# Local and global attention with a routed expert layer on one core: the split weights as sixteen tiles, expert 1's loads in quarters, and two changes in the attention's order

## The chip, the cores and the metric

The kernel is one program on one core of a Trainium2 chip. The metric is the device time of one execution in microseconds, taken as the median of several runs. A profile of one execution was taken besides; its times are counted from the first instruction of the span.

## The reference, cut to what matters

Attention of 8 batches and 8 heads with 512 local and 32 global rows per head gives x, 4352 rows of 512. Each row of x goes to one of 8 experts, chosen by the largest logit against `expert_emb`:

```python
out_g = np.matmul(sm(s_g), v_all)                 # globals look at all keys
a_l = sm(np.concatenate([s_lg, s_ll], axis=-1))   # locals: the globals and a window of 32 either side
x = attn_out.transpose(0, 2, 1, 3).reshape(B * S, H * D)
...
expert_idx = np.argmax(logits, axis=1)
for e in range(E):
    mask = expert_idx == e
    h = np.maximum(x[mask] @ w1[e], 0.0)
    out[mask] = gate_w[mask, None] * (h @ w2[e])
```

`w1[e]` is 512x1024 and `w2[e]` is 1024x512, all in float32.

## The kernel before, in words

**Attention and routing.** 32 steps, four for each batch. Every step has a slot in a plan (`at(g, phase, ...)`, L886 to L968): in slot g the phases are carried out in the order of the numbers at L890, apart from a few that `slot` (L999) puts elsewhere. TensorE computes scores, transposes and values; VectorE the row maxima (`maxima`, L525) and the normalisation of a step's values into x (`normed`, L589 to L597: three instructions on the PSUM tile `po`); ScalarE the exponentials and the copies. The globals' part of a batch is `g_scores`, `g_exps`, `g_turned`, `g_take` and `g_values` (L600 to L682); `g_values` ends in three VectorE instructions (L672 to L675) that wait for TensorE. GpSimd scatters the finished rows of x into the DRAM table `xs`, ordered by expert, and the last rows of each expert's part are filled up by `fill_rest` (L1121): expert 0's from SyncE's queue (SP), the seven others from GpSimd's. Two blocks of 128 rows of expert 0 are computed early with plain float32 matmuls (`early_block`, L200).

**The expert stage.** The remaining rows are worked in items of 128 rows of one expert (`item`, L1276); 36 of them ran in the profiled execution. Float32 products are made from two parts: a rounded part H and the rest L, of the weights (`WH`, `WL`) and of the activations (`xH`/`xL`, `hH`/`hL`), and three matmuls for each (HH, HL, LH). `WH` and `WL` were one tile each, [128, 4, 4096]: two experts by two halves (w1, w2). ScalarE casts `stg` into `WH` and VectorE subtracts it to get `WL`, in pieces of 512 columns (`w_parts`, L1293); one half, 8 pieces, for each item, for the expert that comes next. `first_parts` (L1206) does the same for expert 0 in pieces of 1024 columns. Where a piece's place is known only at run time, its address comes from a register (`ds(ra, 1)`), and the framework that sets the semaphores then orders it by tiles.

An item w is, in TensorE's order: `up(0)` and `up(1)`, 12 matmuls of 128x128x512 each (x times w1, two halves of h), then the two `down`, 12 matmuls each, of the item before it. h needs a transpose through DRAM: ScalarE makes relu (`relu`, L1252) and puts it to `hd` with a DMA of its own queue (`put_h`, L1259), SP loads it back as `hq` (`get_h`, L1263), VectorE turns it in 32x32 blocks into `hk` (L167), and ScalarE and VectorE split it into `hH` and `hL`. An expert's weights come into two stages, `stg0` for w1 and `stg1` for w2, by `load_w` (L1226) with two DMAs of 1 MB on SP's queue, some of which are skipped by a condition. SP's queue is in the order of the program: what waits at its head holds up all behind it. Items 0, 1 and 2 and the rest have orders written out by hand (L1341 to L1391). At the end `declare_no_dep` takes out the orders between the two slots that the framework can't see.

Of the kernel before, what the change touches and what calls it, by code (L numbers as in the profile page):

```python
# [107 lines left out]
def tile_kernel(ctx: ExitStack, tc: tile.TileContext, qk, va, emb, tau, wraw, cst, out):  # L108
# [29 lines left out]
    xT1 = const.tile([P, DM], F32, name="xT1")  # L138
    sums = [const.tile([P, 4 + NE], F32, name=f"ce{i}") for i in range(4)]
# [60 lines left out]
    def early_block(x, h, hT, ob, acc, acc2):  # L200


        def turn(src):
            o = acc()
            for c in range(4):
                transpose(o[:, c * P : (c + 1) * P], src[:, c * P : (c + 1) * P], ident)
            return o

        st = {}

        def begin(xT):
            st["xT"] = xT
            turn_blocks(xT[:, :DM], x[:, :DM])

        def up(nh, ks):
            if ks[0] == 0:
                st["g", nh] = acc()
                if nh == 0:
                    st["h"], st["hT"] = h(), hT()
            for k in ks:  # L220
                c = k * 1024 + nh * 512
                matmul(
                    st["g", nh], st["xT"][:, k * P : (k + 1) * P], cols(st0[0], c, c + 512), start=(k == 0), stop=(k == 3)
                )
            if ks[-1] == 3:
                nc.scalar.activation(st["h"][:, nh * 512 : (nh + 1) * 512], st["g", nh], AF.Relu)

        def half(nh):
            nc.scalar.copy(st["hT"][:, nh * 512 : (nh + 1) * 512], turn(st["h"][:, nh * 512 : (nh + 1) * 512]))

        def down(ks):
            if ks[0] == 0:
                st["g2"] = acc2()
            for k in ks:
                matmul(
                    st["g2"],
                    st["hT"][:, k * P : (k + 1) * P],
                    cols(st0[1], k * 512, (k + 1) * 512),
                    start=(k == 0),
                    stop=(k == 7),  # L240
                )
# [21 lines left out]
        lambda: hq,  # L263
# [5 lines left out]
    with ExitStack() as actx:  # L269
# [634 lines left out]
        for b in range(NB):  # L904
# [116 lines left out]
        def fetch_early():  # L1021
# [5 lines left out]
            for i, x in enumerate((eb[0], xn1)):  # L1027
# [5 lines left out]
                    lambda: eb[3],  # L1033
# [68 lines left out]
    wp.tile([P, 104], F32, name="gap_wp")  # L1102
    WH = wp.tile([P, 4, 4096], F32R, name="WH")
    WL = wp.tile([P, 4, 4096], F32R, name="WL")
    WH2 = WH.rearrange("p (s h) n -> p s (h n)", s=2)
    WL2 = WL.rearrange("p (s h) n -> p s (h n)", s=2)

# [3 lines left out]
    hq = hp.tile([P, DF], F32, name="hq")  # L1111
    hqs = [hq[:, :DM], hq[:, DM:]]
# [6 lines left out]
    firsts = []  # L1119

    def fill_rest(e):  # L1121

        eng = nc.gpsimd if e else nc.sync
        r = eng.value_load(runi[:1, e : e + 1], min_val=e * CAP, max_val=e * CAP + NT)
        ins = eng.dma_start(xs[ds(r, P), :], fill)
        for f in fills + scat + early + (firsts if e else []):
# [79 lines left out]
    def first_parts(hf, c):  # L1206

        cs = slice(c * 1024, (c + 1) * 1024)
        src = cols(st0[hf], cs.start, cs.stop)
        nc.scalar.copy(WH[:, hf, cs], src)  # L1210
        nc.vector.tensor_tensor(WL[:, hf, cs], src, WH[:, hf, cs], ALU.subtract)

# [13 lines left out]
    def load_w(w):  # L1226
        r = entry(nc.sync, 1, w, 2 * NE - 1)
        src = wraw[ds(r, 1), :, :].rearrange("a p (c n) -> p (a c) n", n=WRUN)
        for n in range(2):
            cs = slice(2 * n, 2 * n + 2)  # L1230
            new = {} if w < 2 else {"cond": entry(nc.sync, 4 + n, w, 1)}
            nc.sync.dma_start(st0[w % 2][:, cs, :WRUN], src[:, cs, :], **new)

# [42 lines left out]
    def item(w, pend):  # L1276
# [9 lines left out]
        if w == 0:  # L1286
            todo = []
        elif w == 1:
            todo = [(*held[0], c) for c in range(8)] + [(*held[1], c) for c in range(3)]
        elif w == 2:  # L1290
            todo = [(*held[1], c) for c in range(3, 8)] + todo

        def w_parts(n):  # L1293
            for _ in range(min(n, len(todo))):
# [7 lines left out]
        def product(o, a, W, col, start=False, stop=False):  # L1302
            return nc.tensor.matmul(o.unsqueeze(1), a, W[:, ds(rp, 1), col : col + 512], start=start, stop=stop)  # L1303

        def up(nh):
            g = ps_1.tile([P, 512], F32, name="g1")
            for k in range(4):
                col = k * 1024 + nh * 512
                reads.append(product(g, xH[:, k, :], WH2, col, start=k == 0))
                reads.append(product(g, xH[:, k, :], WL2, col))  # L1310
                reads.append(product(g, xL[:, k, :], WH2, col, stop=k == 3))
# [4 lines left out]
        def down(nh):  # L1316
# [3 lines left out]
            for k in ks:  # L1320
                made.append(product(g, hH[:, k, :], WH2, 4096 + k * 512, start=k == 0))
                made.append(product(g, hH[:, k, :], WL2, 4096 + k * 512))
            for k in ks:
                made.append(product(g, hL[:, k, :], WH2, 4096 + k * 512, stop=k == 7))
# [16 lines left out]
        if w == 0:  # L1341
            load_w(1)
            send_h(0, ga)
            send_h(1, up(1))
            get_h(w, 0)
            get_h(w, 1)
        elif w == 1:
            w_parts(2)
            send_h(0, ga)
            w_parts(1)  # L1350
# [4 lines left out]
            w_parts(1)  # L1355
            send_h(1, gb)
            get_h(w, 0)
            turn_h(1)
# [3 lines left out]
            w_parts(4)  # L1362
            load_w(w + 1)
            w_parts(3)
            get_h(w, 1)
            reads.extend(pend["down"](1))
        else:
# [15 lines left out]
            if w == 2:  # L1383
                w_parts(2)
                load_w(w + 1)
# [10 lines left out]
        for i, (v, c, m) in enumerate(made):  # L1396
            for u, d, o in last_made + made[:i]:
                if o.ins.engine != m.ins.engine and ((v - u) % 2 or (v == u and c != d)):
                    tc.declare_no_dep(m.ins, o.ins, reason="another half or other columns")
# [17 lines left out]
    with tc.manual_schedule():  # L1417
        nc.vector.tensor_copy(runi, run[:1])
        fill_rest(0)
        for w in range(2):  # L1420
            firsts.extend(load_x(w))
        for e in range(1, NE):
            fill_rest(e)
        tab["tab"], nitem = table()
        parts = [(hf, c) for hf in range(2) for c in range(4)]
        for i, f in enumerate(block):
            if i:
                f()
            for _ in range((2, 0, 1, 0, 1, 1, 0, 2, 0, 0, 0)[i]):
                first_parts(*parts.pop(0))  # L1430
            if i == 8:
                load_w(0)
                turn_x(0)
                split_x(0)
                first_parts(*parts.pop(0))
                turn_x(1)
                split_x(1)
        pend = {}
# [96 lines left out]
```

## Time and profile before

| | us |
|---|---|
| median of 3 runs | 712.75 |
| the runs | 713.24, 708.89, 712.75 |
| the profiled execution | 715.34 |
| its span, first to last instruction | 713.7 |
| TensorE busy | 648.0 (91%) |
| VectorE busy | 541.4 (76%) |
| ScalarE busy | 471.3 (66%) |

The profiled execution took 715.34 us, of which 1.6 lie outside its span. Its stages, by the first matmul of each: attention to about 237 us, the routing's end and the early blocks to 273, items 0 to 3 to 327, items from the fifth on to 685, and the last item with its output to the end. Busy TensorE doesn't mean TensorE at its peak: matmuls overlap, and what counts is the distance from one start to the next. In the timeline's rows a bracket holds the idle time ahead of the row and what ended it; "ACTq" and "SPq" are DMA issues; the chain of waits goes back from the last instruction and gives, in order of time, what each step waited for.

### The profile page before, as it was taken

How to read it: one execution, taken by the hardware profiler on the slowest of the kernel's cores; microseconds unless marked ns; L12 is line 12 of the kernel's file. 1: busy time of each engine (PE TensorE's matmuls, PEld its weight loads, DVE VectorE, ACT ScalarE, POOL GpSimd, SP SyncE). 2: the span in 40 equal slices, each digit the busy share in tenths (PEclk: the TensorE clock that was granted, in tenths of full speed). 3: DMA queues.
4: the chain of work that ended last, by engine and by line, in shares of the span. 5: the costliest groups of instructions: out<-in, count | busy, mean ns of one | idle time of the engine just before them, and what ended most of it. 6: DMA issues, size and time to landing. Idle time of an engine off the chain costs nothing.

```text
span 713.7 us, 23574 instructions
## 1 busy us (share of the span) xinstructions
PE 648.0 (91%) x7423; PEld 497.4 (70%) x7425; DVE 541.4 (76%) x1716; ACT 471.3 (66%) x954; POOL 96.6 (14%) x179
## 2 busy tenths in 40 slices
PE   8789879878887899779999999999999999998994
PEld 4567667656676546657777787777878787776783
DVE  2758779789777684778888888787888878867882
ACT  4676767758667244667777776777777776766771
POOL 2011122122212350000100101010110101010101
PEclk9899999999999899889999999999999999999998
DMA  8898899879899259765545577678777787764451
GB/s 258 308 255 257 260 286 275 259 238 297 274 278 290 78 191 313 213 216 167 159 135 144 137 256 202 197 232 255 239 214 208 229 259 220 228 191 128 136 150 40
DMA packets 125148, 154.71 MB, mean 217 GB/s; under 512 B 15881, under 2 KB 81545, under 8 KB 125016
## 3 DMA queue, kind: packets, MB, share of 16 engines
q1 hardware_dynamic: 80680, 114.48, 54.3%
q10 hardware_dynamic: 38016, 18.88, 9.0%
q0 software_dynamic: 6320, 19.71, 7.5%
q8 instruction: 69, 1.13, 0.6%
q14 instruction: 63, 0.52, 0.2%
HBM read 161.36 MB, written 40.94 MB: 283 GB/s over the span
## 4 chain that ended last, share of the span: by engine, by line
PE 37%; DVE 19%; DMA 14%; ACT 12%; issue 11%; ACTq 3%; SPq 2%; DVEq 1%; POOL 0%; another core or an unknown queue 0%; POOLq 0%
DVE WL L1299 14%; PE g L1303 10%; PE pt L198 8%; PE po L195 7%; ACT WH L1298 6%; DMA hd<-h 6%; PE pt L195 6%; PE s_ps L195 5%; ACT h L1253 4%; DMA hq<-hd 3%; DMA raw<-in_qk_dram 3%; ACTq L1261 3%; DMA stg<-in_wraw_dram 1%; DVE hk L167 1%; SPq L1220 1%
## 5 line engine op out<-in xcount | busy, mean ns | idle before, releaser
L1299 DVE TENSOR_TENSOR WL<-stg,WH 128x512 f32 (+1 forms) x288 | 197.8, 689 | 65.0 <-ACT WH L1298 50.2
L1298 ACT CAST WH<-stg 128x512 f32 (+1 forms) x288 | 177.6, 620 | 41.9 <-ACT h L1253 35.2
L1303 PE MATMUL g<-WL,xH 128*128 (+1 forms) x288 | 117.8, 409 | 8.7 <-DVE WL L1299 6.7
L1303 PE MATMUL g<-WH,hH 128*128 (+1 forms) x288 | 114.3, 397 | 10.0 <-ACT hH L1235 10.0
L1303 PE MATMUL g<-WH,xH 128*128 (+1 forms) x288 | 114.3, 397 | 4.4 <-ACT WH L1298 4.3
L1303 PE MATMUL g<-WH,xL 128*128 (+1 forms) x288 | 114.0, 396 | 0.0
L1303 PE MATMUL g<-WL,hH 128*128 (+1 forms) x288 | 114.0, 396 | 0.0
L175 POOL DMA_INDIRECT out_dram<-ob x37 | 36.0, 974 | 407.6 <-DVE xk L167 354.7
L552 ACT ACTIVATE pb<-pb,nm 128x128 f32<-128x128 f32 x256 | 80.1, 395 | 11.0 <-DVE nm L535 11.0
L1303 PE MATMUL g<-WH,hL 128*128 (+1 forms) x288 | 78.1, 393 | 0.0
L1303 PEld LDWEIGHTS g<-WL,xH 128*128 128x128 f32 x288 | 55.1, 191 | 32.7 <-DVE WL L1299 22.0
L1303 PEld LDWEIGHTS g<-WH,hH 128*128 128x128 f32 x288 | 55.2, 192 | 22.8 <-ACT hH L1235 6.5
L1303 PEld LDWEIGHTS g<-WH,xH 128*128 128x128 f32 x288 | 55.0, 191 | 18.9 <-ACT WH L1298 6.2
L1303 PEld LDWEIGHTS g<-WL,hH 128*128 128x128 f32 x288 | 55.2, 192 | 11.5
L1303 PEld LDWEIGHTS g<-WH,hL 128*128 128x128 f32 x288 | 55.0, 191 | 11.7
L1303 PEld LDWEIGHTS g<-WH,xL 128*128 128x128 f32 x288 | 55.3, 192 | 10.9 <-DVE xL L1236 0.4
L195 PE MATMUL s_ps<-raw 64*32 64x128 f32 (+1 forms) x1792 | 49.6, 287 | 12.5 <-issue 7.9
L167 DVE STREAM_TRANSPOSE hk<-hq 128x512 f32<-128x512 f32 x72 | 50.3, 698 | 12.7 <-DMA hq<-hd 8.9
L195 PE MATMUL po<-vt,pT 128*32 128x65 f32 x2048 | 46.1, 231 | 11.0 <-issue 9.7
L1235 ACT CAST hH<-hk 128x512 fp32r<-128x512 f32 x72 | 44.5, 618 | 14.9 <-DVE hk L167 14.6
L564 ACT COPY pT<-pt 128x512 f32<-128x512 f32 x64 | 34.4, 588 | 28.2 <-PE pt L198 28.0
L1253 ACT ACTIVATE h<-g 128x512 f32<-128x512 f32 x72 | 43.0, 597 | 14.7 <-PE g L1303 12.9
(200 smaller groups left out, 879.3 us busy)
## 6 DMA issues: line engine op xcount, KB each, us to landing
stg<-in_wraw_dram SPq DMA_DIRECT2D x74, 1024.0 KB
vt<-in_va_dram SPq DMA_DIRECT2D x96, 260.0 KB
hd<-h ACTq DMA_DIRECT2D x72, 256.0 KB
hq<-hd SPq DMA_DIRECT2D x72, 256.0 KB
raw<-in_qk_dram SPq DMA_DIRECT2D x56, 304.0 KB
xr<-xs SPq DMA_DIRECT2D x152, 64.0 KB
vt<-in_va_dram SPq DMA_DIRECT2D x32, 130.0 KB
stg<-in_wraw_dram SPq DMA_DIRECT2D x16, 256.0 KB
```

Of the source, the lines that this page charges most:

```text
L167: nc.vector.transpose(xT.rearrange("p (k t n) -> p t k n", k=4, t=4), x.rearrange("p (t k n) -> p t k n", t=4, k=4))
L175: nc.gpsimd.indirect_dma_start(out=out[:, :], out_offset=bass.IndirectOffsetOnAxis(ap=ob[:, DM : DM + 1].bitcast(U32), axis=0), in_=ob[:, ...
L195: return counted(nc.tensor.matmul(out, lhsT, rhs, start=start, stop=stop), 4 if lhsT.dtype == F32 else 2)
L198: return counted(nc.tensor.transpose(out, in_, eye), 2)
L552: nc.scalar.activation(pb[:, cs], pb[:, cs], AF.Exp, bias=nm[:, n : n + 1], scale=-1.0)
L564: nc.scalar.copy(pT, state["tp", g, grp])
L1235: nc.scalar.copy(tH, x)
L1253: nc.scalar.activation(hs[nh].rearrange("p (g k n) -> p k g n", g=4, k=4), g.rearrange("p (k g n) -> p k g n", k=4, g=4), AF.Relu,)
L1261: nc.scalar.dma_start(hd, hs[nh].rearrange("p (g n) -> p g n", g=4))
L1298: a = nc.scalar.copy(WH[:, ds(ra, 1), cs], s3)
L1299: b = nc.vector.tensor_tensor(WL[:, ds(rv, 1), cs], s3, WH[:, ds(rv, 1), cs], ALU.subtract)
L1303: return nc.tensor.matmul(o.unsqueeze(1), a, W[:, ds(rp, 1), col : col + 512], start=start, stop=stop)
```

## The change

`WH` and `WL` become eight tiles each of [128, 4, 512], one per 512 columns (columns of w1 for k = 0..3 and the two halves of h, so that tile c = 2k + nh holds what `up(nh)` reads for k, and `down` reads tile k of w2). `first_parts` goes by 512 columns, tiles 0, 2, 4, 6 first. The declarations at the item's end are cut accordingly. `hq` becomes two tiles. Expert 1's weights come in quarters of 512 KB (`first_w`), the first set ahead of item 0 and the second around item 0's loads of h; item 0 casts four pieces, item 1 eight (eleven before), item 2 twelve (thirteen before); in items 1 and 2 `load_w` stands between the two loads of h. All eight fills stand on SP ahead of the first loads of x. `normed` moves into the phase of `g_values`, ahead of it, and the last copy of the last batch's globals into the phase before. Two spare columns are set anew so that the tiles begin where they did.

```diff
-            at(g + 2, NORM, normed, g)
+            at(g + 2, GVAL, normed, g)
...
-                at(g, LATE, g_take, b, part)
+                at(g, BACK if b == NB - 1 and part == 2 else LATE, g_take, b, part)
...
-    WH = wp.tile([P, 4, 4096], F32R, name="WH")
-    WL = wp.tile([P, 4, 4096], F32R, name="WL")
+    WH = [wp.tile([P, 4, 512], F32R, name=f"WH{c}") for c in range(8)]
+    WL = [wp.tile([P, 4, 512], F32R, name=f"WL{c}") for c in range(8)]
...
-    hq = hp.tile([P, DF], F32, name="hq")
-    hqs = [hq[:, :DM], hq[:, DM:]]
+    hqs = [hp.tile([P, DM], F32, name=f"hq{nh}") for nh in range(2)]
...
-        eng = nc.gpsimd if e else nc.sync
-        r = eng.value_load(runi[:1, e : e + 1], min_val=e * CAP, max_val=e * CAP + NT)
-        ins = eng.dma_start(xs[ds(r, P), :], fill)
+        r = nc.sync.value_load(runi[:1, e : e + 1], min_val=e * CAP, max_val=e * CAP + NT)
+        ins = nc.sync.dma_start(xs[ds(r, P), :], fill)
...
+    def first_w(w, lo, hi):
+        src = wraw[2 + w].rearrange("p (c n) -> p c n", n=WRUN)
+        for n in range(lo, hi):
+            nc.sync.dma_start(st0[w][:, n, :WRUN], src[:, n, :])
...
-                a = nc.scalar.copy(WH[:, ds(ra, 1), cs], s3)
-                b = nc.vector.tensor_tensor(WL[:, ds(rv, 1), cs], s3, WH[:, ds(rv, 1), cs], ALU.subtract)
+                a = nc.scalar.copy(WH[c][:, ds(ra, 1)], s3)
+                b = nc.vector.tensor_tensor(WL[c][:, ds(rv, 1)], s3, WH[c][:, ds(rv, 1)], ALU.subtract)
...
         if w == 0:
-            load_w(1)
             send_h(0, ga)
+            w_parts(2)
             send_h(1, up(1))
             get_h(w, 0)
+            first_w(1, 0, 1)
             get_h(w, 1)
+            first_w(1, 1, 4)
+            w_parts(2)
         elif w == 1:
             w_parts(2)
             send_h(0, ga)
-            w_parts(1)
+            w_parts(2)
             turn_h(0)
             split_h(0)
             gb = up(1)
             reads.extend(pend["down"](0))
-            w_parts(1)
             send_h(1, gb)
             get_h(w, 0)
+            load_w(w + 1)
             turn_h(1)
             split_h(1)
             turn_x(w + 1)
             split_x(w + 1)
             w_parts(4)
-            load_w(w + 1)
-            w_parts(3)
             get_h(w, 1)
...
-        fill_rest(0)
-        for w in range(2):
-            firsts.extend(load_x(w))
-        for e in range(1, NE):
+        for e in range(NE):
             fill_rest(e)
+        load_x(0)
+        load_x(1)
...
             if i == 8:
-                load_w(0)
+                first_w(0, 0, 4)
```

On SP, in items 0 and 1 (`hd_58`, `hd_59` are the halves of item 0's h, `stg_90` is w2's stage before, `hq` what VectorE turns), before:

```order
L158 DMA gt_5757<-xs 128x1x2
L1232 DMA stg_90<-in_wraw_dram 128x2x1024 x2
L1264 DMA hq<-hd_58 128x512
L1264 DMA hq<-hd_59 128x512
L1220 TENSOR_LOAD tab
```

and now (w2's stage is `stg_91`, in four pieces):

```order
L159 DMA gt_5772<-xs 128x1x2
L1265 DMA hq_5776<-hd_58 128x512
L1233 DMA stg_91<-in_wraw_dram 128x1024
L1265 DMA hq_5777<-hd_59 128x512
L1233 DMA stg_91<-in_wraw_dram 128x1024 x3
L1216 TENSOR_LOAD tab
```

Both loads of h have moved ahead of all but a quarter of w2's load.

On TensorE, at the start of a later item's `up(0)`, with the semaphores that each row waits for (another engine's name: that engine has got so far), before:

```order
L1303 MATMUL g1_6675<-WH_5751,xH1_5766 128x512 [waits PE_49,Activation_49]
...
L1303 MATMUL g1_6675<-WL_5752,xH1_5766 128x512 [waits DVE_49]
...
L1303 MATMUL g1_6675<-WH_5751,xL1_5768 128x512
...
L1303 MATMUL g1_6675<-WH_5751,xH1_5766 128x512
...
L1303 MATMUL g1_6675<-WL_5752,xH1_5766 128x512
```

and now:

```order
L1305 MATMUL g1_6711<-WH0_5752,xH1_5782 128x512 [waits PE_49]
...
L1305 MATMUL g1_6711<-WL0_5760,xH1_5782 128x512
...
L1305 MATMUL g1_6711<-WH2_5754,xH1_5782 128x512 [waits Activation_49]
...
L1305 MATMUL g1_6711<-WL2_5762,xH1_5782 128x512 [waits DVE_49]
...
L1305 MATMUL g1_6711<-WH4_5756,xH1_5782 128x512 [waits Activation_49]
```

One wait each for ScalarE and VectorE at the item's first two matmuls has become pairs of waits at tiles 2, 4 and 6, and another pair at tile 7 in `up(1)`. (VectorE's own row for a piece of `WL` waited for VectorE and ScalarE, with two register instructions ahead; now it waits for ScalarE alone, with one.)

On VectorE, in an attention slot with `g_values` (`rs`, `xt` are `normed`'s, `rg`, `on` those of `g_values`), before:

```order
L672 TENSOR_SCALAR rg<-pt 128x1
L673 RECIPROCAL rg<-rg 128x1
L675 TENSOR_SCALAR on<-pt,rg 128x64
L594 TENSOR_SCALAR rs<-po 128x8
L595 RECIPROCAL rs<-rs 128x8
L597 TENSOR_TENSOR xt_163<-po,rs 128x4x4x32
```

and now:

```order
L595 TENSOR_SCALAR rs<-po 128x8
L596 RECIPROCAL rs<-rs 128x8
L598 TENSOR_TENSOR xt_164<-po,rs 128x4x4x32
L673 TENSOR_SCALAR rg<-pt 128x1
L674 RECIPROCAL rg<-rg 128x1
L676 TENSOR_SCALAR on<-pt,rg 128x64
```

The normalisation has moved ahead of the three instructions that wait for the globals' matmuls.

## Rows read from the trace of the kernel before

**Rows 1.** Stretches: us, busy time (instructions) by engine, PEclk, DMA share, GB/s.
```profile
236.60:273.00 36.40, 36.24 (x192) 18.29 (x192) 28.14 (x118) 15.55 (x25) 14.52 (x19) 0.94 0.49 152
273.00:326.90 53.90, 44.74 (x168) 35.33 (x169) 35.63 (x57) 31.45 (x54) 2.99 (x3) 0.87 0.74 236
326.90:685.50 358.60, 349.22 (x1490) 277.92 (x1489) 292.19 (x466) 256.06 (x434) 30.12 (x31) 1.00 0.66 197
```

**Rows 2.** Chain of waits within one item: start us, us, what.
```profile
361.84 2.80 PE g L1303 x11
...
369.22 0.70 DVE WL L1299
...
373.15 0.50 PE g L1303
```

**Rows 3.** Timeline of TensorE, items 0 to 4.
```profile
272.97 0.50 PE L1303 MATMUL g<-WH,xH 128*128 128x512 f32 x1
...
289.65 0.79 PE L1303 MATMUL g<-WH,hH 128*128 128x512 f32 x1 [5.23 <-ACT hH L1235]
...
297.94 0.39 PE L1303 MATMUL g<-WH,xH 128*128 x1
...
303.38 0.39 PE L1303 MATMUL g<-WH,hH 128*128 128x512 f32 x1
...
311.53 0.50 PE L1303 MATMUL g<-WH,xH 128*128 x1 [2.55 <-ACT WH L1298]
313.42 0.79 PE L1303 MATMUL g<-WL,xH 128*128 x1 [1.39 <-DVE WL L1299]
...
326.94 0.39 PE L1303 MATMUL g<-WH,xH 128*128 x1
```

**Rows 4.** Timeline of VectorE: seven pieces at fixed places, five at places from a register.
```profile
294.84 4.30 DVE L1299 TENSOR_TENSOR WL<-stg,WH 128x512 fp32r<-128x512 f32 x7
...
369.22 3.88 DVE L1299 TENSOR_TENSOR WL<-stg,WH 128x512 f32 x5 [0.81 <-ACT WH L1298]
```

**Rows 5.** Timeline of ScalarE in the item of rows 2.
```profile
364.67 0.60 ACT L1253 ACTIVATE h<-g 128x512 f32<-128x512 f32 x1 [0.27 <-PE g L1303]
...
368.57 3.23 ACT L1298 CAST WH<-stg 128x512 f32 x5 [0.54 <-ACT h L1253]
```

**Rows 6.** Chain of waits, whole span: start us, us, what.
```profile
277.50 6.88 DMA hd<-h
...
327.39 2.80 PE g L1303 x11
...
444.79 7.21 DMA hd<-h
452.06 2.33 DMA hq<-hd
...
464.25 5.50 DMA stg<-in_wraw_dram
470.90 2.80 DMA hd<-h
...
685.98 2.79 PE g L1303 x11
```

**Rows 7.** Timeline of SP's queue around items 0 and 1.
```profile
254.25 0.39 SPq L1125 DMA_DIRECT2D xs<-fill  x1
263.54 2.17 SPq L156 DMA_DIRECT2D xr<-xs  x4
...
276.25 4.64 SPq L1232 DMA_DIRECT2D stg<-in_wraw_dram  x2
284.44 3.48 SPq L1264 DMA_DIRECT2D hq<-hd  x2
```

**Rows 8.** Waits, whole span: who, for whom, us in total, times, longest us.
```profile
DVE rg L672 <- PE pt L195: 16.9, 12, 2.7
...
PE pt L198 <- DVE lg L748: 3.1, 1, 3.1
```

More of the change, by code (lines that the diff above doesn't have):

```diff
@@ L138, in tile_kernel @@
     xT1 = const.tile([P, DM], F32, name="xT1")
+    const.tile([P, 8], F32, name="gap_c")
     sums = [const.tile([P, 4 + NE], F32, name=f"ce{i}") for i in range(4)]
@@ L228, in half @@
         def half(nh):
-            nc.scalar.copy(st["hT"][:, nh * 512 : (nh + 1) * 512], turn(st["h"][:, nh * 512 : (nh + 1) * 512]))
+            nc.scalar.copy(st["hT"][nh], turn(st["h"][:, nh * 512 : (nh + 1) * 512]))
         def down(ks):
@@ L1118, in tile_kernel @@
     fills = []
[L1119 removed]
     def fill_rest(e):
[L1123 to L1126 removed]
+        r = nc.sync.value_load(runi[:1, e : e + 1], min_val=e * CAP, max_val=e * CAP + NT)
+        ins = nc.sync.dma_start(xs[ds(r, P), :], fill)
+        for f in fills + scat + early:
             tc.declare_no_dep(ins.ins, f.ins, reason="disjoint rows")
@@ L1206, in first_parts @@
     def first_parts(hf, c):
[L1208 to L1211, printed above, removed]
+        src = cols(st0[hf], c * 512, (c + 1) * 512)
+        nc.scalar.copy(WH[c][:, hf], src)
+        nc.vector.tensor_tensor(WL[c][:, hf], src, WH[c][:, hf], ALU.subtract)
     last_made = []
@@ L1286, in item @@
         if w == 0:
-            todo = []
+            todo = todo[:4]
         elif w == 1:
-            todo = [(*held[0], c) for c in range(8)] + [(*held[1], c) for c in range(3)]
+            todo = [(*held[0], c) for c in range(4, 8)] + [(*held[1], c) for c in range(4)]
         elif w == 2:
-            todo = [(*held[1], c) for c in range(3, 8)] + todo
+            todo = [(*held[1], c) for c in range(4, 8)] + todo
         def w_parts(n):
@@ L1307, in up @@
             for k in range(4):
[L1308 to L1311, printed above, removed]
+                c = 2 * k + nh
+                reads.append(product(g, xH[:, k, :], WH2[c], 0, start=k == 0))
+                reads.append(product(g, xH[:, k, :], WL2[c], 0))
+                reads.append(product(g, xL[:, k, :], WH2[c], 0, stop=k == 3))
             return g
@@ L1362, in item @@
             w_parts(4)
+            get_h(w, 1)
+            reads.extend(pend["down"](1))
+        elif w == 2:
+            turn_x(w + 1)
+            turn_h(0)
+            split_x(w + 1)
+            split_h(0)
+            turn_h(1)
+            send_h(0, ga)
+            w_parts(2)
+            split_h(1)
+            gb = up(1)
+            reads.extend(pend["down"](0))
+            send_h(1, gb)
+            w_parts(2)
+            get_h(w, 0)
             load_w(w + 1)
-            w_parts(3)
+            w_parts(8)
             get_h(w, 1)
@@ L1397, in item @@
             for u, d, o in last_made + made[:i]:
-                if o.ins.engine != m.ins.engine and ((v - u) % 2 or (v == u and c != d)):
-                    tc.declare_no_dep(m.ins, o.ins, reason="another half or other columns")
+                if c == d and (v - u) % 2:
+                    tc.declare_no_dep(m.ins, o.ins, reason="another half")
         last_made[:] = made
@@ L1418, in tile_kernel, with slices @@
         nc.vector.tensor_copy(runi, run[:1])
-        fill_rest(0)
-        for w in range(2):
-            firsts.extend(load_x(w))
-        for e in range(1, NE):
+        for e in range(NE):
             fill_rest(e)
+        load_x(0)
+        load_x(1)
         tab["tab"], nitem = table()
-        parts = [(hf, c) for hf in range(2) for c in range(4)]
+        parts = [(0, c) for c in (0, 2, 4, 6, 1, 3, 5, 7)] + [(1, c) for c in range(8)]
+        def slices(n):
+            for _ in range(n):
+                first_parts(*parts.pop(0))
         for i, f in enumerate(block):
@@ L1428, in tile_kernel @@
                 f()
-            for _ in range((2, 0, 1, 0, 1, 1, 0, 2, 0, 0, 0)[i]):
-                first_parts(*parts.pop(0))
+            slices((4, 0, 2, 0, 2, 2, 0, 0, 0, 0, 0)[i])
             if i == 8:
-                load_w(0)
+                first_w(0, 0, 4)
                 turn_x(0)
                 split_x(0)
-                first_parts(*parts.pop(0))
+                slices(2)
                 turn_x(1)
                 split_x(1)
+                slices(4)
         pend = {}
```

26 lines of the change are left out of this document (12 added, 14 removed).

## The prediction

> **What bounds the kernel now.** I read the table of stretches first [rows 1]: from 326.9 to the end of the items TensorE is busy in 349.22 of 358.6 us at a full granted clock. That looks like a bound, but busy time counts stalled matmuls too, so I looked at distances from start to start. Where nothing holds it, TensorE does 24 matmuls in 303.38 − 297.94 = 5.44 us [rows 3], 0.227 each; an item has 48, so it could take 10.88. The 31 items between the starts at 327.39 and 685.98 [rows 6] took 358.6/31 = 11.57 each, and the undisturbed one of [rows 2], from 361.84 to 373.15, took 11.31. So TensorE loses 0.69 per item, 21.3 us in all, and the stage's limit is something else.
>
> The chain inside one item [rows 2] says what: `up(0)`, then the casts, then the last piece of `WL` at the end of the run that starts at 369.22, and only behind it the next item's first matmul, at 373.15. In [rows 4] that run of five ends at 373.10, 0.05 before. Since `WL` is one tile, the next `up(0)` waits for the eighth piece though it reads the first. ScalarE's relu at 364.67 waited in turn for TensorE [rows 5]. This is a ring: `up(0)` → relu → `WH` → `WL` → `up(0)`.
>
> Two smaller losses lie ahead of it. From 273 to 326.9 the granted clock is 0.87, a mean over its two levels (1.2 and 2.4 GHz) [rows 1], and TensorE stands 5.23 us until h's first part comes [rows 3]; seven half items of 5.44 (38.1) take 54.0. In the attention VectorE waits 16.9 us in 12 places for the globals' matmuls, while TensorE's wait for VectorE at the routing is 3.1 once [rows 8].
>
> **The change part by part.** The profiled execution took 715.34, of which 713.7 are span; the median is 712.75. I make the sum against 715.34 and take 2.6 off.
>
> *Sixteen tiles, steady items.* `up(0)` reads tiles 0, 2, 4 and 6, three matmuls (0.68) each. The seven pieces of [rows 4] start (4.30 − 0.69)/6 = 0.60 apart; call the end of piece 7 T. Piece 6 is ready at T − 0.6 and wanted 2.04 behind the item's start, piece 4 at T − 1.8 and wanted at 1.36, piece 2 at T − 3.0 and wanted at 0.68. The item may start at the latest of T − 2.64, T − 3.16 and T − 3.68: 2.6 us sooner than now, and only 0.4 are needed to close the gap to 10.88. The ring through ScalarE, with its idle 0.27 gone, is 11.31 − 0.27 = 11.04 if nothing else changes. `WL` also loses its wait for VectorE itself and one register instruction. At register places the pieces now start (3.88 − 0.69)/4 = 0.80 apart, at fixed places 0.60; ScalarE's `WH` (3.23 − 0.62)/4 = 0.65. With 0.60 to 0.65 four steps give back 0.6 to 0.8, and the ring is 10.2 to 10.4, under TensorE's 10.88.
>
> The rows show that pieces without a wait on their own engine start 0.60 apart though each lasts 0.69, so the wait and the registers are the 0.20 [rows 4]. Against that stands the Trainium skill, VectorE: DVE Perf Modes, section "The DRAIN you can't avoid": the next operation can't issue until the pipe is empty, and a semaphore behind each operation "costs nothing extra". By it the step would stay 0.80 and the ring 11.04, which would take 31 × 0.16 = 5 us off the gain; the trace disagrees, with 0.60.
>
> What remains above 10.88 is h's trip through DRAM. When no weights are loading, `hd` takes 2.80; when they are, 7.21, with `hq` 2.33 behind [rows 6]. With relu, turn and split at 0.6 to 0.7 each that is an estimated 11.7, some 0.8 more than an item has. If this strikes once for each of the six later experts it is 5 us, 0.16 an item. So 11.04 per item and 31 × 0.53 = 16.5 us gained. Bounds: 21.3 if TensorE never waits, 12 if the slow items keep the 0.26 that they have above 11.31 now (31 × (11.57 − 11.18), with a little for restarts).
>
> *Items 0 to 3.* Now 2 MB stand on SP before h's loads: `stg` issued at 276.25, `hq` only at 284.44 [rows 7], and the first `hd` takes 6.88 [rows 6]. Then both loads of h go ahead of most of w2. With 2.80 and 2.33 for 6.88 and 3.48, h is there 5.2 sooner, which would end all of the 5.23 idle; as w1's quarters are still in flight I leave 1.3, a gain of 3.9. Without that stop the clock shouldn't fall: the stretch from 289.65 to 297.94 [rows 3] becomes 5.44 for 8.29, gain 2.85. Item 1's second half took 311.53 − 303.38 = 8.15, 2.55 of it waiting for `WH`; by tiles it would be 5.44, gain 2.7. From 311.53 to 326.94 are 15.4 us for 10.88, gain 4.5. Together 14. The casts are no fewer (32 pieces before item 3), so I take 12; the lower bound is 4, the idle time alone. The fifth item would start near 315 instead of 326.94.
>
> *Quarters.* Four DMAs of 512 KB for two of 1 MB. The nearest row is one 1 MB piece, 5.50 [rows 6]; four quarters that ran one behind another at that would be 22 us and late (rival B); overlapping like the pair at 276.25 [rows 7] they cost SP two more issues, hidden, as SP only waits then. I take nothing; worst 8 us. By the Trainium skill, DMA: Bandwidth & Descriptors, section "Measured (HBM→SBUF, 128 partitions, SWDGE, issued from GpSimd)", DMAs should be batched to 1 MiB or more; no row here has a 512 KB weight load, and my sum does not lean on the rule.
>
> *The fills on SP.* Seven more, each one issue (0.39 [rows 7]) and a register load, about as much again: 5.5 to 6 us behind 254.25, so done by 261. SP's next, the loads of x, issue at 263.54 since they wait for the scatter [rows 7]: hidden, though the last fill must also land within the 2.5 us left. Without that cover 2 to 3 us. GpSimd loses the same work off the path.
>
> *First parts by 512.* Eight more instructions on ScalarE and VectorE, beside TensorE that is busy 36.24 of 36.40 [rows 1]: nothing, 1 us at worst.
>
> *`normed` ahead of the globals' operations.* Three instructions, none added; they run in time in which VectorE waits anyway (12 places, 16.9 us [rows 8]). TensorE gains only where VectorE is late for it, so I take 2 us, between 0 and the 3.1 of [rows 8] with some for smaller waits, 4. The earlier copy of the globals, the two `hq` tiles and the spare columns: nothing, 0.5 either way; before, the second `hq` load waited on the first tile's reader, which is gone.
>
> The sum: 16.5 + 12 + 2 = 30.5, and 0.3 at the last item: 715.34 − 30.8 = 684.5; against the median 682. I lean one up, since at least one edit's cost is usually missed: **683**.
>
> **The rivals.** *A: the ring keeps the pace.* Casts, relu and h's loads are as many as before; if the `WL` step stays 0.80 and the slow items keep their 0.26, an item takes 11.04 + 0.26 = 11.30. Gain 8.4 + 12 + 2.3 = 22.7: 692.6, against the median 690. For it: ScalarE is busy 292 of 358.6 and stands in the ring. Against it: 2.6 us of new slack. *B: w2 of expert 1 comes late.* At 5.50 a quarter the four, started near 283, end at about 305, later than two at 276.25 would; item 3 then waits for casts as now, and the second term falls from 12 to 4: 692.5, 690. For it: `hd` of 6.88 shows that transfers crowd each other here. Against: both loads are the same bytes. *C, slower: the waits chop TensorE.* `up` has eight waits more than now. A matmul that was held shows 0.50 or 0.79 where a free one shows 0.39 [rows 3]: 0.11 to 0.40 for each. If casts arrive just behind TensorE, each wait ends last. With p per wait the item is 11.04 + 8p; the terms ahead of the stage give 14.3, so the kernel is slower from 8p = 0.53 + 0.46, p over 0.12. At 0.15 it is 12.24: 31 × 0.67 − 14.3 = 6.5 slower, 719. Against it: waits that are long satisfied should not hold, and the slack of 2.6 says that they are. *D: the fills delay the loads of x* by 2 to 3 us: 685.5.
>
> **How the numbers follow.** Forecast 0.62, D inside it 0.08 more; A 0.14, B 0.12, C 0.04. All terms at their upper bounds give 715.34 − 21.3 − 14 − 4 − 0.3 = 675.7, the median 673; all at their lower, 12 + 4, less 3 for D, 702, the median 700. A and B lie inside. The range is 673 to 699. About 1% is what a measurement of this kernel can tell from no change, so "faster" is below 705.6: everything but C and a doubled A with B. Faster 0.92, same 0.04, slower 0.04.
>
> **What would show it.** Right: TensorE's start-to-start for an item is 10.9 to 11.1; the item's first `WL` matmul is not released by the last piece of `WL`; a run of `WL` pieces starts 0.60 apart; `hq` is issued before the last three quarters of w2, the idle time before item 0's `down` is under 2 us and the clock does not fall there; the fifth item starts near 315; SP's loads of x still issue at 263.5, and the first expert matmul comes about 2 us sooner. Wrong: 11.3 per item (A); a wait for `stg` in item 2 or 3 (B); many short waits of TensorE for ScalarE and VectorE inside `up` (C); loads of x after 265 (D).

## The result: 691.4 us, 3.0% faster, nearly all of it from the tiles

The changed kernel took 691.43 us as the median of four runs (684.72 to 694.49), the kernel before 712.07 beside it: a ratio of 0.970, interval 0.962 to 0.979. A second set gave 691.42 against 712.74, 0.970 (0.964 to 0.977). The forecast was 683 in a range of 673 to 699: sign and range held, but 30 us of gain were expected and about 21 came. The profiled execution took 689.40 with a span of 687.5. Runs more than 1.5% above the fastest of their kernel count in the medians but not in the ratios, and the profiles of `backward`, `h_first` and `turn_early`, being of such runs, are read below for single waits alone.

TensorE's timeline in the changed kernel (items 0 to 3, one later item, the last item's start), with the brackets as in [rows 3]:

```profile
266.67 0.79 PE L1305 MATMUL g<-WH,xH 128*128 128x512 f32 x1
...
281.63 0.50 PE L1305 MATMUL g<-WH,hH 128*128 128x512 f32 x1 [3.48 <-ACT hH L1236]
...
295.76 0.50 PE L1305 MATMUL g<-WH,hH 128*128 128x512 f32 x1 [1.32 <-ACT hH L1236]
...
301.55 0.50 PE L1305 MATMUL g<-WH,hH 128*128 128x512 f32 x1 [2.77 <-ACT hH L1236]
...
317.40 0.39 PE L1305 MATMUL g<-WH,xH 128*128 x1
...
360.98 0.39 PE L1305 MATMUL g<-WH,xH 128*128 x1
...
371.86 0.39 PE L1305 MATMUL g<-WH,xH 128*128 x1
...
658.63 0.39 PE L1305 MATMUL g<-WH,xH 128*128 x1
```

From 360.98 to 371.86 is 10.88: TensorE's own pace. The 31 items from 317.40 to 658.63 took 11.01 each (before 11.57). The first matmul of the expert stage came at 266.67 (before 272.97), the fifth item 50.7 us behind it (before 54.0). The stretches, with columns as in [rows 1]:

```profile
266.67:317.40 50.73, 42.23 (x170) 32.29 (x169) 35.48 (x60) 31.40 (x58) 2.92 (x3) 0.97 0.80 248
317.40:658.60 341.20, 338.63 (x1489) 278.77 (x1488) 278.84 (x468) 241.81 (x436) 30.20 (x31) 1.00 0.71 208
281.60:288.80 7.20, 7.17 (x24) 5.75 (x25) 5.79 (x10) 3.80 (x7) 0.00 (x0) 0.76 0.85 282
```

TensorE's 338.63 of 341.20 busy are no longer stalls: 31 items of 10.88 are 337.3. The third row is item 0's `down`, at a granted clock of 0.76, a mean over the two levels (1.2 and 2.4 GHz). VectorE's timeline, at the first turning of h and in the later item:

```profile
279.01 1.29 DVE L1300 TENSOR_TENSOR WL<-stg,WH 128x512 fp32r<-128x512 f32 x2 [0.61 <-ACT WH L1299]
280.22 0.70 DVE L168 STREAM_TRANSPOSE hk<-hq 128x512 f32<-128x512 f32 x1
...
368.39 3.10 DVE L1300 TENSOR_TENSOR WL<-stg,WH 128x512 f32 x5 [0.80 <-ACT WH L1299]
```

ScalarE at item 0's first half of h, and in the later item:

```profile
269.46 2.18 ACT L1206 CAST WH<-stg 128x512 fp32r<-128x512 f32 x4
...
272.13 0.58 ACT L1254 ACTIVATE h<-g 128x512 f32<-128x512 f32 x1
272.74 0.39 ACTq L1262 DMA_DIRECT2D hd<-h  x1
...
363.90 0.60 ACT L1254 ACTIVATE h<-g 128x512 f32<-128x512 f32 x1 [0.31 <-PE g L1305]
...
367.74 2.71 ACT L1299 CAST WH<-stg 128x512 f32 x5 [0.52 <-ACT h L1254]
```

Five `WL` pieces take 3.10 where [rows 4] have 3.88: (3.10 − 0.69)/4 = 0.60 from start to start, for 0.80. `WH` goes from 3.23 [rows 5] to 2.71, 0.52 apart. The last piece is done at 371.49, 10.5 behind the item's start, 0.4 ahead of the next. The chain of waits of the start, and of one late item:

```profile
277.95 9.82 DMA hd<-h
...
293.45 6.59 DMA hq<-hd
...
576.37 5.89 DMA hd<-h
582.33 2.59 DMA hq<-hd
```

SP's queue there:

```profile
248.65 10.66 SPq L1122 DMA_DIRECT2D xs<-fill  x8
261.09 1.77 SPq L157 DMA_DIRECT2D xr<-xs  x4
...
276.24 0.36 SPq L1265 DMA_DIRECT2D hq<-hd  x1
276.65 0.41 SPq L1233 DMA_DIRECT2D stg<-in_wraw_dram  x1
277.24 0.33 SPq L1265 DMA_DIRECT2D hq<-hd  x1
277.66 1.57 SPq L1233 DMA_DIRECT2D stg<-in_wraw_dram  x3
280.25 8.45 SPq L157 DMA_DIRECT2D xr<-xs  x4
...
289.62 0.37 SPq L1265 DMA_DIRECT2D hq<-hd  x1
291.77 1.56 SPq L1228 DMA_DIRECT2D stg<-in_wraw_dram  x2
293.45 0.35 SPq L1265 DMA_DIRECT2D hq<-hd  x1
```

Item 0's h is now fetched at 276.24 and 277.24, [rows 7] had 284.44; counted from the first matmul of the stage that is 9.57 us for 11.47. But item 1's put, started at 277.95 into three quarters of w2, takes 9.82; the x load behind the quarters holds SP until 288.7; and the second load of item 1's h goes out behind two megabytes and takes 6.59. Most of the wait for item 0's h (3.48 of 5.23) has stayed, and one for item 1's has come.

### The profile page after: what moved, and what is told of

The parts are those of the page before. It is cut to its first block, busy times and chain, and to the rows that moved or that the text cites. A ratio compares the mean times of both kernels' runs of the same rounds, so it can differ in the third digit from the quotient of the medians.

```text
span 687.5 us, 23125 instructions
## 1 busy us (share of the span) xinstructions
PE 627.8 (91%) x7425; PEld 492.7 (72%) x7425; DVE 525.4 (76%) x1724; ACT 455.0 (66%) x962; POOL 94.9 (14%) x172
## 4 chain that ended last, share of the span: by engine, by line
PE 68%; DMA 9%; DVE 8%; issue 8%; ACT 4%; SPq 1%; ACTq 1%; POOL 0%; DVEq 0%; another core or an unknown queue 0%; POOLq 0%
PE g L1305 45%; PE pt L199 7%; PE po L196 6%; PE pt L196 6%; PE s_ps L196 4%; DMA xr<-xs 2%; DMA hd<-h 2%; DMA raw<-in_qk_dram 2%; DMA hq<-hd 1%; ACT WH L1299 1%; DVE pb L536 1%; DMA xs<-xt,si 1%; DVE WL L1300 1%; DVE xt L598 1%; ACT pb L553 1%
## 5 line engine op out<-in xcount | busy, mean ns | idle before, releaser
L1300 DVE TENSOR_TENSOR WL<-stg,WH 128x512 f32 (+1 forms) x288 | 184.7, 684 | 37.3 <-ACT WH L1299 36.8
L1299 ACT CAST WH<-stg 128x512 f32 (+1 forms) x288 | 163.6, 618 | 37.1 <-ACT h L1254 36.0
L1305 PE MATMUL g<-WL,xH 128*128 (+1 forms) x288 | 112.5, 391 | 0.9 <-DVE WL L1300 0.9
L1305 PE MATMUL g<-WH,xH 128*128 (+1 forms) x288 | 112.5, 391 | 0.0
L1305 PE MATMUL g<-WH,xL 128*128 (+1 forms) x288 | 112.1, 389 | 0.0
L1305 PEld LDWEIGHTS g<-WH,xH 128*128 128x128 f32 x288 | 54.1, 188 | 11.4 <-ACT xH L1236 0.2
L1305 PEld LDWEIGHTS g<-WH,xL 128*128 128x128 f32 x288 | 54.0, 188 | 11.1
L196 PE MATMUL s_ps<-raw 64*32 64x128 f32 (+1 forms) x1792 | 46.2, 280 | 11.4 <-issue 7.4
L536 DVE CUSTOM_DVE_ANT_0 pb<-s_ps,mask 128x128 f32<-128x128 f32 x192 | 44.2, 286 | 13.4 <-PE s_ps L196 13.4
L196 PE MATMUL po<-vt,pT 128*32 128x65 f32 x2048 | 41.7, 230 | 13.4 <-issue 12.9
L1236 ACT CAST xH<-xk 128x512 fp32r<-128x512 f32 x37 | 22.9, 619 | 45.3 <-DVE xk L168 45.2
```

The source lines that it names most:

```text
L196: return counted(nc.tensor.matmul(out, lhsT, rhs, start=start, stop=stop), 4 if lhsT.dtype == F32 else 2)
L536: nc.vector.tensor_tensor_reduce(state["pb", g][grp][:, cs], ps[:, grp, cs], mk, -ISQ, 3.0e38, ALU.add, ALU.min, nm[:, n : n + 1],)
L1236: nc.scalar.copy(tH, x)
L1299: a = nc.scalar.copy(WH[c][:, ds(ra, 1)], s3)
L1300: b = nc.vector.tensor_tensor(WL[c][:, ds(rv, 1)], s3, WH[c][:, ds(rv, 1)], ALU.subtract)
L1305: return nc.tensor.matmul(o.unsqueeze(1), a, w3, start=start, stop=stop)
```

## The experiments

The table is read from each kernel's own profile: the start of the expert stage, the time from there to the fifth item, the mean of the 31 items behind it, and how many of these took over 0.3 more than the median one (10.88, but 11.31 before and 11.32 in `one_tile`). Ratios go against the kernel before on the same chip.

| kernel | median us | ratio (interval) | stage starts | to fifth item | mean item | late |
|---|---|---|---|---|---|---|
| before | 712.07 | | 272.97 | 53.97 | 11.57 | 8 |
| changed | 691.43 | 0.970 (0.962, 0.979) | 266.67 | 50.73 | 11.01 | 3 |
| `again` | 691.42 | 0.970 (0.964, 0.977) | 269.09 | 49.47 | 11.12 | 5 |
| `tiles_only` | 691.78 | 0.972 (0.966, 0.977) | 268.40 | 48.37 | 11.10 | 7 |
| `one_tile` | 714.00 | 1.005 (1.001, 1.009) | 268.91 | 55.15 | 11.61 | 8 |
| `normed_back` | 694.76 | 0.973 (0.968, 0.979) | 270.90 | 49.20 | 11.07 | 6 |
| `casts_early` | 693.59 | 0.976 (0.971, 0.982) | 273.23 | 45.69 | 11.12 | 3 |
| `xr_first` | 708.60 | 0.993 (0.989, 0.997) | 266.89 | 48.50 | 11.59 | 6 |
| `no_w2` | 690.74 | 0.972 (0.966, 0.978) | 273.72 | 44.91 | 11.14 | 6 |
| `split_load` | 692.98 | 0.976 (0.971, 0.980) | 271.60 | 46.99 | 11.28 | 9 |
| `split_early` | 692.19 | 0.976 (0.971, 0.981) | 272.45 | 47.72 | 11.15 | 5 |
| `backward` | 697.06 | 0.977 (0.970, 0.984) | | | | |
| `h_first` | 690.75 | 0.965 (0.959, 0.971) | | | | |
| `turn_early` | 693.76 | 0.973 (0.967, 0.979) | | | | |

**The kernel again.**

> The changed kernel itself once more, for a tighter time and a second profile. If the profiled execution (26 us below that of before) tells the true gain, 686 to 690 us and a ratio of 0.964 to 0.970; if the four timed runs do (20.6 us), 691 and 0.970. In the trace: items of 10.88 us but for a few late ones; the stretch from item 0's first matmul to the fifth item's near 47.6 us if what holds it there is fixed by the order, elsewhere if it is chance.

It gave 691.42: the timed runs told the gain, not the one profiled execution, which was among the quicker ones. The stretch to the fifth item took 49.5 us, with a put of 9.80 at the same place. The order alone doesn't fix that loss, though: `split_load`, below, has the changed kernel's orders ahead of item 3, and in its profile the stretch took 47.0, without the loss at item 1's h. There the put went out 0.79 ahead of the three quarters, and not within 0.3 of the first as in the changed kernel, `again`, `normed_back` and `xr_first`. Whether the loss hangs on that was not tried. ScalarE, then SP, then SP's wait for the put, all in `split_load`:

```profile
282.36 0.37 ACTq L1262 DMA_DIRECT2D hd<-h  x1
...
283.15 1.79 SPq L1233 DMA_DIRECT2D stg<-in_wraw_dram  x3
285.96 3.59 SPq L157 DMA_DIRECT2D xr<-xs  x4
...
SPq L157 <- DMA hd<-h: 1.0, 1, 1.0
```

In the changed kernel the same wait for the put is 6.1, in `again` 5.9.

**The tiles alone, and all but the tiles.** `tiles_only` takes the two tiles of the kernel before apart and keeps its orders:

```diff
-    WH = wp.tile([P, 4, 4096], F32R, name="WH")
-    WL = wp.tile([P, 4, 4096], F32R, name="WL")
+    WH = [wp.tile([P, 4, 512], F32R, name=f"WH{c}") for c in range(8)]
+    WL = [wp.tile([P, 4, 512], F32R, name=f"WL{c}") for c in range(8)]
...
-                if o.ins.engine != m.ins.engine and ((v - u) % 2 or (v == u and c != d)):
+                if c == d and (v - u) % 2:
```

> The kernel before with the sixteen tiles alone; loads, casts, fills and attention as before. By my theory (the wait for the last piece and for its own engine set the item) items take 10.88 to 11.0 us and the 31 items give back about 17 us; the stretch from item 0 to the fifth item keeps its 5 us wait for h and gains 1 to 4 us: 691 to 695 us. By the rival that the order of items 0 to 2 and the loads carry the gain and the tiles only help them: 705 or more, items of 11.3 or more.

`one_tile` is the changed kernel with these lines the other way round:

```diff
-    WH = [wp.tile([P, 4, 512], F32R, name=f"WH{c}") for c in range(8)]
+    WHt = wp.tile([P, 4, 4096], F32R, name="WH")
...
-                if c == d and (v - u) % 2:
+                if o.ins.engine != m.ins.engine and ((v - u) % 2 or (v == u and c != d)):
```

> The changed kernel with WH and WL as one tile each, as before, and the old declarations; all else changed. By my theory items take 11.5 us again, VectorE's pieces start 0.80 apart, and the time is 691 plus 31 x 0.65 = 20 us less what it keeps at the start: 706 to 712. By the rival that the tiles matter little once loads and casts are in their new order: 691 to 697.

`tiles_only` gave 691.78, within 0.4 us of the whole change; `one_tile` gave 714.0, no better than before (its interval lies just above 1) and 2 above its expectation, as it kept nothing at the start (55.15 us to the fifth item). So the tiles are the gain, and the other edits together gain nothing that can be measured, with the tiles or without. VectorE's rows say why: first `tiles_only`,

```profile
367.81 3.10 DVE L1298 TENSOR_TENSOR WL<-stg,WH 128x512 f32 x5 [0.81 <-ACT WH L1297]
```

then `one_tile`, whose pieces are 0.80 apart again,

```profile
354.55 3.88 DVE L1301 TENSOR_TENSOR WL<-stg,WH 128x512 f32 x5 [0.84 <-ACT WH L1300]
```

and its TensorE, which waits again for the last piece before the second matmul of an item, here 0.23 us:

```profile
347.21 0.50 PE L1306 MATMUL g<-WL,xH 128*128 x1 [0.23 <-DVE WL L1301]
```

**The two halves of the tile term.** `backward`:

```diff
-            for k in range(4):
+            for k in (3, 2, 1, 0):
```

> The changed kernel, but up goes through its tiles from the last to the first (k = 3, 2, 1, 0), so an item's first matmul needs tile 6, the last but one of the pieces made. It tells the two halves of the tile term apart. If the pieces' shorter spacing (0.60 for 0.80) is enough, the last piece is ready 10.5 us behind the item's start as in the changed kernel's trace, the wait is over before TensorE comes, and items stay at 10.88: same time, 689 to 692. If the 2.6 us of slack from reading the tiles in the order in which they are made is needed, items take 11.1 to 11.4: 697 to 707.

697.06, at the lower edge of the second expectation, with an interval that overlaps that of the changed kernel: not decided. The median item still took 10.88, though an item now begins with the last piece but one; TensorE had seven waits for `WL` again, 3.3 us in all, and in this profile, 7.1 us above the median time, 11 of the 31 items were late. The shorter spacing is enough for an item in which nothing is late. Whether the slack is worth the 5.6 us (4.8 by the ratios) stays open.

**`normed`.** The one line of the plan put back:

```diff
-            at(g + 2, GVAL, normed, g)
+            at(g + 2, NORM, normed, g)
```

> The changed kernel with normed back in its old phase, behind the globals' operations; nothing else. By my forecast's term it loses the 2 us that the move gave (0 to 4): 691 to 695, the first expert matmul 2 us later. By the rival that VectorE's waits only changed owner (the wait for the globals' matmuls fell from 16.9 to 3.8 us, but normed now waits 12.1 us for the values' matmuls): no change, 690 to 692.

694.76, 3.3 above the changed kernel (2.3 by the ratios) with intervals that overlap: undecided. The waits changed owner, as the view of waits in the changed kernel shows:

```profile
DVE rs L595 <- PE po L196: 12.1, 12, 2.7
...
DVE rg L673 <- PE pt L196: 3.8, 5, 1.5
```

Together 15.9 us where [rows 8] had 16.9 for `rg`; in the same view before, `rs` waited 8.8 us for `po` besides, so the sum fell, but that alone doesn't show that TensorE was done sooner. The start of the expert stage can't decide it either: it lies at 272.97 and 268.40 in two kernels with the old attention, and from 266.67 to 273.72 in those with the new.

**Item 0 to 3: what holds h.** `no_w2` leaves expert 1's w2 out:

```diff
-            first_w(1, 0, 1)
             get_h(w, 1)
-            first_w(1, 1, 4)
```

> The changed kernel without the four quarters of expert 1's w2 (2 MB that are not loaded at all; the rows of expert 1 are computed with other numbers): what do these transfers cost at the start of the expert stage? If the put and load of item 1's h (9.8 us for the put in both profiles) are slow because the quarters are in flight: the put takes about 3 us, TensorE's two waits ahead of item 1's down (1.3 and 2.8) go, the stretch to the fifth item falls from 50 to 45 us or less, 4 to 6 us faster: 686. If SP's order or the casts hold them: the stretch stays near 50 and the time at 690 to 692.

44.9 us to the fifth item: both waits ahead of item 1's `down` are gone, every half item from x2 on takes 5.44. Only this is left on TensorE:

```profile
288.62 0.79 PE L1305 MATMUL g<-WH,hH 128*128 128x512 f32 x1 [3.42 <-ACT hH L1236]
```

So the wait for item 0's h does not come from w2's transfers; that item 1's does fits this profile and the put of 9.82, but `split_load` lost nothing at item 1's h with the transfers in place. The whole time, at 690.74, did not follow the 5 us; its interval and that of the changed kernel, some 4 and 6 us either way, are too wide to tell. `h_first` changes SP's order instead:

```diff
             get_h(w, 1)
+            load_x(3)
             first_w(1, 1, 4)
...
             get_h(w, 0)
-            load_w(w + 1)
...
             get_h(w, 1)
+            load_w(w + 1)
```

> The changed kernel with SP's order at items 0 and 1 mended by the chain of its trace: the load of x for item 3 goes ahead of the last three quarters of w2, and item 2's weights go behind both loads of item 1's h (in the changed kernel SP stands at that x load from 280 to 288 and the second load of h takes 6.6 us behind 2 MB of weights). If SP's order is what holds item 1's h: TensorE's waits ahead of its two halves (1.3 and 2.8 us) go, the stretch from item 0 to the fifth item falls from about 50 to 46 us, 4 us faster in all, 687. If the transfers themselves are the limit (put and load of h share the engines with the quarters, 9.8 us for one put): the waits stay within 1 us of what they were and the time does not move, 690 to 692; the weights may then be late for item 2 instead, 692 to 695.

690.75, not told apart from the changed kernel. The two waits at item 1 went, but its profile has new ones, of 1.84 and 2.86, one and two items later. `casts_early` adds:

```diff
             turn_x(w + 1)
-            turn_h(0)
             split_x(w + 1)
+            w_parts(4)
+            turn_h(0)
```

> As the run before, and item 2 casts the four pieces left of w2 ahead of the turning of item 1's h, where ScalarE stands idle for some 6 us in the changed kernel's trace. If item 3's up waits for casts because ScalarE's order puts ten of them behind that h (four waits of 0.24 and TensorE at half pace, 2.1 us): these go, 1 to 2 us less than the run before. If they wait for the weights to land: no gain, or 1 us slower as h comes later.

Item 3's four waits for casts went. The stretch fell to 45.7, 5 less than in the changed kernel, yet the time is 693.59. In this profile the next item gives 2.3 of it back: the chain of waits of `casts_early` behind the stretch,

```profile
306.70 5.42 DMA stg<-in_wraw_dram
...
313.81 6.81 DMA hd<-h
```

SP's queue,

```profile
312.42 8.53 SPq L157 DMA_DIRECT2D xr<-xs  x4
```

and TensorE, in the middle of an item that takes 13.23:

```profile
326.56 0.50 PE L1305 MATMUL g<-WH,hH 128*128 x1 [2.04 <-ACT hH L1236]
```

It is the same picture one load later: weights, a put that is slow among them, SP standing at an x load until the put has landed, h late. `turn_early` goes for item 0's wait:

```diff
             send_h(0, ga)
-            w_parts(2)
             turn_h(0)
             split_h(0)
+            w_parts(2)
```

> The changed kernel; in item 1 the turning and splitting of item 0's h goes ahead of the second pair of casts and not behind it. TensorE's wait ahead of item 0's down was 3.5 us in the changed kernel and 3.4 without the transfers of w2, so the weights in flight don't make it. If the casts that stand ahead of the turning on VectorE do (VectorE turns the first h at 280.2 with no idle time, right behind two pieces that start at 279.0): the wait falls by 1.2 to 1.6 us, to about 2, and the low clock of item 0's down (0.76) may go with it, 1 to 3 us. If h is not there sooner: the wait stays at 3.4.

The wait was 2.33, but it varies without this edit too: 3.48 in the changed kernel, 2.60 in `again`, 2.69 to 3.53 in `normed_back`, `xr_first` and `split_load`. From the issue of h's load to its turning it is 2.65 us here and 3.14 to 4.04 in those five, so VectorE's order costs 0.5 to 1.4; the turning now waits 0.94 for the transfer itself. The granted clock of item 0's `down` was 1.00, but so it was in `again`. The time, 693.76, shows no gain.

**Late items.** `xr_first`:

```diff
-        if w > 2 and w + 1 < NI:
-            load_w(w + 1)
         if w + 2 < NI:
             load_x(w + 2)
+        if w > 2 and w + 1 < NI:
+            load_w(w + 1)
```

> The changed kernel with the load of x ahead of the load of weights in every item from the fourth on; nothing else. In the two profiles of the changed kernel 3 to 5 items of 31 are late by 0.4 to 3.9 us, with an x load of 5 to 6 us behind 2 MB of weights in the chain, ahead of the turning of h on VectorE. If that x load is the cause: late items go or halve, the mean item is 10.88 to 10.95, 3 to 5 us faster, 687 to 688. If h's own trip through DRAM is the cause, as forecast: no change, 690 to 692.

My x load theory fell: 708.6, 17 us slower than the changed kernel. The chain of waits at its worst item,

```profile
569.12 7.99 DMA hq<-hd
```

SP's queue, where the weights now go out right ahead of the loads of h,

```profile
567.25 1.77 SPq L1228 DMA_DIRECT2D stg<-in_wraw_dram  x2
569.12 0.95 SPq L1265 DMA_DIRECT2D hq<-hd  x2
```

and TensorE, in an item of 18.18:

```profile
578.62 0.79 PE L1305 MATMUL g<-WH,hH 128*128 x1 [4.43 <-ACT hH L1236]
```

The late x loads of the changed kernel were, as far as this shows, a sign of the same two megabytes. `split_load` parts them:

```diff
-            load_w(w + 1)
+            load_w(w + 1, (0,))
...
             get_h(w, 1)
+            if w + 1 < NI:
+                load_w(w + 1, (1,))
```

> The changed kernel with the second megabyte of each weight load, from the fourth item on, issued behind the item's loads of h and not ahead of them. By the theory that late items are h's trip through DRAM behind 2 MB of weights: fewer and smaller late items, mean item 10.88 to 10.95 (now 11.01 to 11.12), 3 to 5 us faster, 686 to 689. By the rival that moving the megabyte only moves the collision to the next item's loads, or brings the weights late as with the x load ahead of them: 692 or more, with new late items.

Nine late items and 692.98: the collision moved, as the rival said. With `casts_early` it is `split_early`:

> The same split together with the edits of casts_early, whose stretch to the fifth item took 45.7 us but whose next item was 2.4 late behind a load of weights and a put of 6.8 us. If that load is why its gain was given back: stretch near 46, no late item behind it, 682 to 687, below both kernels. If not: 690 to 694.

692.19, 47.7 us to the fifth item. No version here is measurably faster than the changed kernel.

## Why the prediction was right in sign and its gain nearly half too large

**Steady items, 16.5 us: right, and so was the chain behind it.** 358.55 became 341.23 in one profile and 344.81 in the other, 17.3 and 13.7 us. The ring was read rightly (a wait for the last piece, pieces that wait on their own engine), but for one row: the matmul at 373.15 is the item's second, the first that reads `WL`. The first had started before the last piece was done, in the kernel before:

```profile
372.63 0.39 PE L1303 MATMUL g<-WH,xH 128*128 x1
```

Undisturbed items fell to 10.88 sharp. What is left above that, 0.13 and 0.24 for the 0.16 taken, fits h's trip behind weights, as said: the only waits of TensorE in the 31 items of the changed kernel are three for h, 2.6 us of the 3.9 above 10.88,

```profile
PE g L1305 <- ACT hH L1236: 2.6, 3, 1.7
```

and in `again` four, 3.6 of 7.5, the longest with a load of weights and one of h ahead of it in the chain. The emphasis was wrong in one point: the prediction stood on the 2.6 us of slack, but the pieces' spacing alone brings the last piece to 10.5, under 10.88. The Trainium skill (VectorE: DVE Perf Modes, section "The DRAIN you can't avoid") has a semaphore after each operation cost "nothing extra", from which the prediction took a step of 0.80; the same section says that an operation that is not held starts earlier, and with that the 0.60 between pieces of 0.69 agrees. In `one_tile`, which waits for its own engine and runs one more register instruction, the step is 0.80. In the chain of waits of the kernel before, 0.10 of the 0.20 lies between a piece's end and the next start, with the register instruction (DVEq) inside:

```profile
369.92 0.03 issue
369.95 0.02 DVEq L1299
369.97 0.04 issue
370.02 0.70 DVE WL L1299
```

The other 0.10 is the overlap of two pieces, which one that waits for the piece before it can't have. How much of the gap the register instruction makes by itself was not separated.

**Items 0 to 3, "so I take 12": the step that failed.** The two profiles show 3.2 and 4.5, three more with the same orders ahead of item 3 (`normed_back`, `xr_first`, `split_load`) 4.8 to 7.0, all against one profile of before. By half items, each at 5.44 without loss, the excess in us is (a wait ahead of a half stands in the column before it):

| | x0, x1 up to h0 | h0 | x2 | h1 | x3 | h2 | sum |
|---|---|---|---|---|---|---|---|
| before | 5.80 | 2.85 | 0 | 2.71 | 4.53 | 0 | 15.9 |
| changed | 4.08 | 1.76 | 1.49 | 3.22 | 2.10 | 0 | 12.7 |
| `again` | 3.21 | 0.14 | 1.40 | 5.85 | 0.79 | 0 | 11.4 |
| `normed_back` | 4.14 | 2.95 | 0 | 1.97 | 2.06 | 0 | 11.1 |
| `xr_first` | 3.27 | 2.98 | 0 | 3.47 | 0.70 | 0 | 10.4 |
| `split_load` | 3.55 | 1.66 | 0 | 0.06 | 3.50 | 0.14 | 8.9 |
| `tiles_only` | 6.85 | 2.47 | 0 | 0 | 0.97 | 0 | 10.3 |
| `one_tile` | 3.69 | 1.76 | 1.78 | 6.03 | 3.81 | 0 | 17.1 |
| `no_w2` | 4.02 | 2.81 | 0 | 0 | 0 | 0 | 6.8 |

The steps of the prediction, one by one:

- "h is there 5.2 sooner, which would end all of the 5.23 idle": its load went out 1.9 sooner, and 3.48 of the idle stayed. Two rows were misread. The 3.48 of [rows 7] is the time in which SP issued two loads, not the time of one load; and the load at 284.44 waited for its own put (277.50 + 6.88 = 284.38), not for the weights ahead of it on SP. The put did get shorter, 3.50 at most (272.74 to 276.24), but it started 6.07 behind the stage's first matmul, before 4.53: on ScalarE four casts of `first_parts` now stand ahead of the relu, a term that the prediction had at nothing, 1 at worst. Then VectorE turns h at 280.22 right behind two pieces that stand ahead of it in its order (0.5 to 1.4, by `turn_early`).
- "Without that stop the clock shouldn't fall": a stop of 3.48 remained, the granted clock of 281.6 to 288.8 was 0.76, and h0 lost 1.76. How long TensorE stood doesn't decide it alone: behind 2.60 in `again` the granted clock of h0 (283.18 to 288.76) was 1.00, behind 2.69 in `xr_first` (281.04 to 289.46) 0.64.
- "By tiles it would be 5.44": true of item 1's casts, in `tiles_only` the h1 and x2 columns are 0; but the new load order, which the prediction counted on, lets item 1's put go out among w2's quarters, and x2 and h1 lose 4.7 again in the changed kernel (7.3, 2.0, 3.5 and 0.06 in the four others).
- "Gain 4.5" for x3: 2.4 came, as four waits of 0.22 to 0.24 for pieces of `WL` stayed in item 3's `up(0)`.

I priced the transfer that was moved ahead and not the one that it was moved ahead of: near rival B's mechanism (0.12), with item 1's h as its first victim and only then the casts. The term came to 3 to 7, around B's 4.

**Attention, 2 us: not decided.** The fills were hidden, but not as said: the eight took 10.66 and not some 6, and the x loads, at 261.09 sooner than the 263.54 of [rows 7] only because this attention ended sooner, came 7.7 us behind the last scatter of x where they had come 4.6 behind it. GpSimd's last scatter, before and then now:

```profile
258.97 0.97 POOL L837 DMA_INDIRECT xs<-xt,si  x1 [0.30 <-DVE e L1174]
...
253.38 0.98 POOL L838 DMA_INDIRECT xs<-xt,si  x1 [0.30 <-issue]
```

So the delay of **D** did come, 3.1 us, but not its cost: the first expert matmul came 13.3 behind that scatter, before 14.0. **C** did not come: `up` has eight waits for casts where there were two (six more, not eight), and in the changed kernel's steady items none of them held TensorE. **Quarters:** `tiles_only` has 1 MB pieces and the same time, though other edits differ with them, so the Trainium skill's advice to batch (DMA: Bandwidth & Descriptors, "Measured (HBM→SBUF, 128 partitions, SWDGE, issued from GpSimd)") decides nothing measurable here. **The last item,** taken as 0.3 sooner, was 0.7 and 1.1 longer: 28.9 and 29.3 for 28.2.

**The sum.** 17.3 + 3.2 − 0.7 = 19.8 without the attention in one profile, 13.7 + 4.5 − 1.1 = 17.1 in the other, 21 measured.

## What to carry to other kernels

A tile is the unit of waiting: where a producer fills a buffer in pieces and the consumer reads it in the same order, one tile for each piece takes away the wait for the last piece and the producer's wait for itself, and the careful moves in the order gave nothing measurable beside that. When a transfer is moved ahead of another in a shared queue, price the one that falls behind, its own put included. A loss of some us that was taken away at the start of the stage could not be found in the whole time: a part came back at the next load of weights (2.3 of 5 in `casts_early`), and the rest is within the spread.

## What the runs showed of the hardware

A put of 256 KB took 2.80 us with no weights loading [rows 6] and 9.82 and 9.80 with quarters of 512 KB in flight beside it; a load of as much took 2.33 [rows 6] and up to 7.99 right behind two megabytes. SP stood for 8.5 us at the issue of four 64 KB loads, by the chain of waits until a put of ScalarE's queue had landed (277.95 + 9.82 = 287.77); this was not tried by itself. And the same attention ended up to 7 us apart from one profile to the next (the stage starts at 266.67 to 273.72 in kernels that differ only behind it), beside a spread of 9.8 between the timed runs (684.72 to 694.49), so that one profile against one profile says little on gains below that.
